# Issuing the loads of v for batches 2 to 7 from ScalarE, with three buffers of their own

## The chip, the cores and the metric

The kernel runs on one core of one Trainium2 chip. The metric is the device time of one execution, in microseconds (us). Profiled executions give a span, from the first to the last instruction; the device time is the span and about 1.7 us.

## The reference

Eight batches, eight heads, 576 positions, 64 features a head, all float32. Attention with a causal mask and a decay bias comes first, then one residual MLP over the joined heads:

```python
scores = scale * q @ k.T                       # per batch and head
cum    = cumsum(max(s, 0))
bias   = min(-(cum[:, None] - cum[None, :]), 0)
attn   = softmax(where(causal, -1e9, scores + bias))
x      = concat_heads(attn @ v)                # [8, 576, 512]
out    = x + relu(layer_norm(x) * g @ w1) @ w2 # 512 -> 2048 -> 512
```

## The kernel before

The kernel is scheduled by hand: every engine runs its instructions in the order in which the program emits them. The program goes through 64 **slots**, one head each. A slot computes the scores of its head, applies the exponential, multiplies with v for the head of two slots before, and fills the rest of TensorE's time with MLP work of the batch before ("units").

v comes in five tiles a batch (four of 128 positions, one of 64). For batches 2 to 7 each tile is loaded as float32 by SyncE and cast to bfloat16 by GpSimd one slot later. k and q of the later batches (rows) go through the same staging buffers: SyncE loads, GpSimd casts, SyncE starts a transposing transfer into `kq`, from which TensorE reads.

```python
stage = ctx.enter_context(tc.tile_pool(name="stage", bufs=6))

def ld_v(b, t):
    ...
    tmp = stage.tile([P, H, D], F32, name="vtmp", tag="st")
    nc.sync.dma_start(
        out=tmp[:pn], in_=v[b, :, t * P : t * P + pn, :].rearrange("h s d -> s h d")
    )
    loaded["v", b, t] = tmp

def cast_v(b, t, eng):                       # on GpSimd, one slot later
    ...
    copy_on(eng, v_bf[b % 2][:pn, t, :, 0:D], loaded.pop(("v", b, t))[:pn])

def ld_rows(gam, t): ...                     # SyncE loads k, q into tag "st"
def tr_rows(gam, t): ...                     # SyncE: dma_start_transpose -> kq

def pre(n):                                  # at the head of slot n
    ...                                      # rows: loads, casts, transposes
    for nb in range(2, B):
        m = n - H * nb + (5 if nb == 2 else 7)
        if 0 <= m < NT:
            ld_v(nb, m)
        if 1 <= m <= NT:
            cast_v(nb, m - 1, "pool")

for n in range(BH):                          # slots from 9 on, cut
    b, h = n // H, n % H
    pre(n)
    ...
    scores(b, h)          # three matmul banks sa, sb, sc; ScalarE Exp after each
    run_units(1, True)    # mlp1: 4 matmuls into ph, then hT by VectorE or ScalarE
    if h % 2 == 0:
        scores_d(b, h // 2)
    run_units(1)
    pv_next()             # attention times v, two slots behind
    ...
    run_units(nu)
```

The softmax here doesn't subtract the row's maximum and nothing guards it: scores larger than these inputs give would overflow.

## Time and profile before

| | before |
|---|---|
| median of the runs given with the kernel | 367.58 us (367.33 to 367.63) |
| profiled execution | 368.54 us, span 366.8 |
| TensorE busy | 355.0 us, 97% of the span |
| loads of v by SyncE | 24 of 256 KB, 6 of 128 KB |
| SyncE's starts of v, shortest / median / longest | 440 / 590 / 1761 ns |

A slot begins with a 512-column matmul into `sa`, so the distance of two such starts is the length of a slot. From slot 24 on, a batch without a stall has slots of 4.63, 4.58, 5.08, 5.02, 4.63, 4.57, 4.63, 4.58 us, and 5.62 in place of 5.02 where the layer norm has a fifth tile. What is over this is a stall.

This is the timeline of TensorE in the kernel before, from 76 to 100 us (start, duration, engine, line, operation, tiles):

```profile
80.58 0.38 PE L312 MATMUL sa<-kq 68*128 68x512 bf16 x1
...
85.20 0.38 PE L312 MATMUL sa<-kq 68*128 68x512 bf16 x1
...
89.78 0.38 PE L312 MATMUL sa<-kq 68*128 68x512 bf16 x1
```

These are slots 20 and 21, of 4.62 and 4.58 us: no stall. (Starts are rounded to 0.01 us, so lengths taken from them can differ by 0.01 from those in the text, which are taken from the unrounded starts.)

### The profile page before, as it was taken

The numbers are of one execution on the slowest core, as the hardware profiler recorded it, in microseconds if no ns is written. First come the engines' busy times: TensorE is split into PE (matmuls) and PEld (weight loads), VectorE is DVE, ScalarE is ACT, GpSimd is POOL, SyncE is SP. The second block draws the span as 40 slices with busy tenths as digits, with TensorE's granted clock in tenths as the row PEclk, the third lists the DMA queues.
The fourth block names the chain that finished last, engine by engine and source line by source line (L and its number), as shares of the span: only waits on it lengthen the run. The fifth ranks groups of instructions, "written<-read, shape, count | busy, mean of one in ns | idle before, by whom it ended". The sixth has DMA issues, their size and how long they took to land.

```text
span 366.8 us, 8315 instructions
## 1 busy us (share of the span) xinstructions
PE 355.0 (97%) x3017; PEld 197.1 (54%) x3067; DVE 202.9 (55%) x535; ACT 191.3 (52%) x367; POOL 164.9 (45%) x447
## 2 busy tenths in 40 slices
PE   8998999999999999999999999999999999999995
PEld 3677555565555555555455555555555554444444
DVE  7697789684357554944384547743675483112211
ACT  5895988467732673367534753476337522501410
POOL 8854468667633656344675563554852101000000
PEclk9999999999999999999999999999999999999999
DMA  8999999999965999599979986798830011011013
GB/s 144 162 195 178 202 211 193 163 240 176 183 146 141 206 199 181 104 215 163 188 176 213 194 183 140 189 191 182 174 102 2 0 59 57 1 58 59 0 31 86
DMA packets 156653, 52.17 MB, mean 142 GB/s; under 512 B 143641, under 2 KB 151940, under 8 KB 156612
## 3 DMA queue, kind: packets, MB, share of 16 engines
q1 hardware_dynamic: 138868, 43.08, 55.5%
q0 software_dynamic: 17344, 8.03, 18.9%
q8 instruction: 24, 0.39, 0.5%
q10 hardware_dynamic: 400, 0.52, 0.4%
q14 instruction: 17, 0.14, 0.2%
HBM read 37.11 MB, written 9.44 MB: 127 GB/s over the span
## 4 chain that ended last, share of the span: by engine, by line
PE 72%; DVE 7%; DMA 6%; SPq 4%; POOL 4%; issue 3%; ACT 3%; POOLq 0%; ACTq 0%
PE py L515 26%; PE ph L497 25%; PE pot L389 6%; SPq L164 3%; PE sc L312 3%; PE sa L312 3%; PE sb L312 3%; DMA rowtmp<-in_q_dram 2%; PE idle L568 2%; DMA vtmp<-in_v_dram 2%; DVE xn L451 2%; PE trx L484 2%; DVE stats L423 1%; POOL er L331 1%; ACT er L323 1%
## 5 line engine op out<-in xcount | busy, mean ns | idle before, releaser
L515 PE MATMUL py<-w_bf,hT 128*128 128x512 bf16 (+1 forms) x565 | 132.1, 373 | 1.6 <-DVE yo L524 0.4
L497 PE MATMUL ph<-xT,w_bf 128*128 128x512 bf16 x478 | 116.4, 379 | 1.1 <-DVE yo L524 0.2
L507 ACT ACTIVATE hT<-ph 128x512 bf16<-128x512 f32 x102 | 61.0, 598 | 64.4 <-PE ph L497 64.4
L515 PEld LDWEIGHTS <-hT 128*128 128x128 bf16 x592 | 53.5, 98 | 49.1 <-issue 0.9
L497 PEld LDWEIGHTS <-w_bf 128*128 128x128 bf16 x560 | 50.1, 97 | 51.3 <-issue 2.9
L323 ACT ACTIVATE er<-sa 128x512 bf16<-128x512 f32 x64 | 38.2, 597 | 70.9 <-PE sa L312 50.1
L331 POOL TENSOR_SCALAR_AFFINE_SELECT er<-er 128x128 bf16<-128x128 bf16 x216 | 59.7, 300 | 22.5 <-ACT er L323 22.3
L505 DVE TENSOR_SCALAR hT<-ph 128x512 bf16<-128x512 f32 x38 | 26.3, 692 | 56.7 <-PE ph L497 49.0
L176 POOL CAST rows<-rowtmp 128x512 bf16<-128x512 f32 (+1 forms) x55 | 33.5, 609 | 50.7 <-DMA rowtmp<-in_q_dram 46.0
L312 PEld LDWEIGHTS <-kq 68*128 68x128 bf16 x452 | 33.4, 97 | 27.4 <-issue 1.7
L389 PEld LDWEIGHTS <-er 128*128 128x128 bf16 x960 | 37.5, 98 | 14.9 <-issue 0.7
L389 PE MATMUL pot<-v_bf,er 128*128 128x65 bf16 x960 | 40.2, 193 | 0.5 <-PE sd L355 0.3
L397 DVE RECIPROCAL rinv<-pot 128x5 f32<-128x5 f32 x64 | 12.3, 192 | 49.2 <-PE pot L389 48.9
L323 ACT ACTIVATE er<-sc 128x512 bf16<-128x512 f32 x64 | 39.2, 612 | 0.0
L323 ACT ACTIVATE er<-sb 128x512 bf16<-128x512 f32 x64 | 38.4, 599 | 0.3 <-PE sb L312 0.2
L524 DVE SCALAR_TENSOR_TENSOR yo<-py,rstd,xb 128x512 f32<-128x512 f32 x32 | 23.9, 748 | 26.2 <-PE py L515 19.7
L399 DVE TENSOR_TENSOR xb<-pot,rinv 128x256 f32<-128x256 f32 x64 | 27.2, 425 | 2.2
L102 POOL CAST v_bf<-vtmp 128x512 bf16<-128x512 f32 (+1 forms) x30 | 18.5, 617 | 19.6 <-DMA vtmp<-in_v_dram 19.5
L439 POOL TENSOR_TENSOR rstd<-rstd,mhalf 128x4 f32<-128x4 f32 (+1 forms) x8 | 8.8, 1095 | 38.0 <-DVE rstd L438 37.9
L312 PE MATMUL sc<-kq 68*128 68x256 bf16 (+1 forms) x216 | 25.3, 229 | 0.3
L423 DVE BATCH_NORM_STATS2 stats<-xb 128x6 f32<-128x128 f32 (+2 forms) x100 | 25.3, 313 | 0.4
L312 PE MATMUL sb<-kq 68*128 68x64 bf16 (+1 forms) x172 | 24.5, 244 | 0.9 <-DMA kq<-rows 0.6
(101 smaller groups left out, 322.1 us busy)
## 6 DMA issues: line engine op xcount, KB each, us to landing
out_dram<-yo SPq DMA_DIRECT2D x32, 256.0 KB
vtmp<-in_v_dram SPq DMA_DIRECT2D x24, 256.0 KB
rowtmp<-in_k_dram SPq DMA_DIRECT2D x44, 128.0 KB
rowtmp<-in_q_dram SPq DMA_DIRECT2D x44, 128.0 KB
w_bf<-in_moe_w_ch_dram POOLq DMA_DIRECT2D x8, 512.0 KB, 10.7
kp<-in_k_dram POOLq DMA_DIRECT2D x9, 144.0 KB, 6.8
qp<-in_q_dram POOLq DMA_DIRECT2D x9, 144.0 KB, 7.0
v_bf<-in_v_dram POOLq DMA_DIRECT2D x8, 128.0 KB, 8.1
```

What stands on the lines that cost most here:

```text
L176: nc.gpsimd.tensor_copy(out=r[0:pn, :, :, 0:D], in_=loaded.pop(("rows", gam, t))[0:pn])
L312: nc.tensor.matmul(a[:, c + a0 - q0 : c + a1 - q0], lhsT=k_cols(b, h, kb), rhs=cols, start=True, stop=not (pe_mask and diag),)
L323: nc.scalar.activation(out=e[:, o : o + 512], in_=a, func=ACT.Exp, scale=scale)
L331: nc.gpsimd.affine_select(out=e[:, o : o + P], in_=e[:, o : o + P], compare_op=ALU.is_ge, fill=0.0, base=0, pattern=[[1, P]], channel_mult ...
L389: nc.tensor.matmul(pot[:, t, :], lhsT=e[:, o : o + P], rhs=vv[:, kb, h, :], start=(kb == 0), stop=(kb == last),)
L399: nc.vector.tensor_tensor(out=xb[b][:, :, hs], in0=pot[:, 0:NF, 0:D], in1=rinv[:, 0:NF].unsqueeze(2).to_broadcast([P, NF, D]), op=ALU.mult,)
L423: nc.vector.bn_stats(out=st[b][:, t, part, :], in_=x[:, lo:hi])
L497: nc.tensor.matmul(ph, lhsT=w1_bf[:, kd, fb * P : (fb + 1) * P], rhs=xT[:, kd, :], start=(kd == 0), stop=(kd == KD - 1),)
L505: nc.vector.tensor_scalar_max(out=hT[:, fb, :], in0=ph, scalar1=0.0)
L507: nc.scalar.activation(out=hT[:, fb, :], in_=ph, func=ACT.Relu)
L515: nc.tensor.matmul(py[0], lhsT=hT[:, fb, t * P : (t + 1) * P], rhs=w2_bf[:, fb, c0:c1], start=(fb == 0), stop=(fb == FB - 1),)
L524: nc.vector.scalar_tensor_tensor(out=yo, in0=py[0], scalar=rs, in1=x[:, c0:c1], op0=ALU.mult, op1=ALU.add)
```

## The change

The intent: take 30 transfer starts from SyncE, whose stream is dense around the transposes of k and q, give them to ScalarE, which is 48% idle, and start the loads sooner, so that GpSimd waits less. The loads get three buffers of their own; `stage`, then for k and q alone, goes from six to four. The casts stay where they are.

```diff
-    stage = ctx.enter_context(tc.tile_pool(name="stage", bufs=6))
+    stage = ctx.enter_context(tc.tile_pool(name="stage", bufs=4))
@@ ld_v
-        tmp = stage.tile([P, H, D], F32, name="vtmp", tag="st")
-        nc.sync.dma_start(
+        tmp = stage.tile([P, H, D], F32, name="vtmp", tag="v", bufs=3)
+        nc.scalar.dma_start(
             out=tmp[:pn], in_=v[b, :, t * P : t * P + pn, :].rearrange("h s d -> s h d")
         )
@@ pre(n)
             m = n - H * nb + (5 if nb == 2 else 7)
-            if 0 <= m < NT:
-                ld_v(nb, m)
             if 1 <= m <= NT:
                 cast_v(nb, m - 1, "pool")
@@ the slot
         scores(b, h)
+        for nb in range(2, B):
+            m = n - H * nb + (5 if nb == 2 else 7)
+            if 0 <= m < NT:
+                ld_v(nb, m)
         run_units(1, True)
```

Below, "the third load" is m = 2 (slots 19, 27, 35, 43, 51 for batches 3 to 7) and "the fifth load" is m = 4 (slots 21, 29, 37, 45, 53).

## The prediction

> **What bounds the kernel now.** I began with the page's busy shares, then read the start of every slot (one head of attention each, 64 in all), the waits around the slots that are too long, SyncE's own stream there, and ScalarE early on. From the page:
>
> ```profile
> PE 355.0 (97%) x3017; PEld 197.1 (54%) x3067; DVE 202.9 (55%) x535; ACT 191.3 (52%) x367; POOL 164.9 (45%) x447
> ```
>
> TensorE is busy 97% of the span, so nothing that only shortens other engines' work moves the end: a change counts only where it opens or closes a gap of TensorE. The page's list of transfers also has 24 loads of v of 256 KB (and 6 of 128 KB), all from SyncE.
>
> Each slot begins with one 512-column score matmul into tile `sa`. The timeline of TensorE from 240 to 262 us, where no stall occurs, and the same view from 160 to 182 us:
>
> ```profile
> 248.21 0.38 PE L312 MATMUL sa<-kq 68*128 68x512 bf16 x1
> ...
> 252.79 0.38 PE L312 MATMUL sa<-kq 68*128 68x512 bf16 x1
> ...
> 257.42 0.38 PE L312 MATMUL sa<-kq 68*128 68x512 bf16 x1
> ```
>
> ```profile
> 170.61 0.38 PE L312 MATMUL sa<-kq 68*128 68x512 bf16 x1
> ...
> 175.95 0.38 PE L312 MATMUL sa<-kq 68*128 68x512 bf16 x1
> ...
> 181.37 0.38 PE L312 MATMUL sa<-kq 68*128 68x512 bf16 x1
> ```
>
> The same two slots of a batch (the last, then the first of the next) take 4.58 and 4.63 us in the first fence, 5.34 and 5.42 us in the second. So 0.76 + 0.79 us is lost there. I laid the other starts from 99 us on beside the same head of the last batch: one more slot is long (4.78 for 4.63, at 156.62 us). Two slots of 5.62 us belong to batches whose layer norm has a fifth tile to transpose; I call those work, not stall. What this part can give back is 0.15 + 0.76 + 0.79 = **1.70 us**.
>
> The waits between 150 and 182 us, largest first in the view, name the stall:
>
> ```profile
> POOL v_bf L102 <- DMA vtmp<-in_v_dram: 3.6, 3, 2.5
> ...
> PEld L312 <- DMA kq<-rows: 1.4, 2, 1.1
> ...
> PEld L389 <- POOL er L331: 0.6, 1, 0.6
> ```
>
> TensorE waits for a transposed tile of k and q (`kq<-rows`), and for a mask that GpSimd (`er`) put on late, because GpSimd, which works in order, stood waiting for a load of v. Both come from SyncE's stream:
>
> ```profile
> 146.33 0.57 SPq L139 DMA_DIRECT2D vtmp<-in_v_dram  x1
> 152.01 0.36 SPq L542 DMA_DIRECT2D out_dram<-yo  x1
> ...
> 167.81 1.73 SPq L139 DMA_DIRECT2D vtmp<-in_v_dram  x1
> 169.66 2.92 SPq L186 DMA_TRANSPOSE kq<-rows  x2
> 172.63 0.62 SPq L139 DMA_DIRECT2D vtmp<-in_v_dram  x1
> 173.67 1.22 SPq L186 DMA_TRANSPOSE kq<-rows  x1
> ```
>
> From 146.9 to 152.0 us SyncE issues nothing: the store of an output tile waits for VectorE, which is in the five tiles of a layer norm. Then it issues almost without a gap until 177 us, and the loads of v stand ahead of the transposes. The transpose that TensorE waits for starts at 173.67, behind a load of v at 172.63 and another at 167.81.
>
> **What the Trainium skill says.** "DMA: Bandwidth & Descriptors", section "Issuing engines are not separate DMA queues": starts from several engines run on the same 16 DMA engines and save only the issuing sequencer's time. The trace can't test it for v yet; but the bytes stay the same, so I count issue time and earlier starts, and no bandwidth. "Perfetto Trace Analysis", section "Sequencer Loop": an engine instruction is pushed into a queue and waits there, while a control instruction is run by the sequencer itself. If a DMA start counts as the latter, part of it hides under an exponential that still runs; no run shows that yet. The same page, section "DMA Instruction — HWDGE (DVE, Sync)": the recorded time of a start is the sequencer's, with a wait for a shared descriptor generator in it, and the movement lies outside. The trace agrees on the last point: the start at 167.81 takes 1.73 us, and the cast that needs its data can run only at 172.37. On sharing, five pairs of stores at the end, from SyncE and ScalarE at once, take 0.47 and 0.50 us each, against 0.36 for a lone store on SyncE: little.
>
> **The change, part by part.**
>
> Removed: 30 starts on SyncE, median 0.59 us (range 0.44 to 1.76) in the view of `vtmp`: 30 x 0.59 = 18 us of SyncE. Between 152 and 174 us four of them take 0.93 + 0.49 + 1.73 + 0.62 = 3.8 us ahead of the late transpose. TensorE waited 1.1 us for it, so that wait should go even if only a third of the 3.8 us is really saved.
>
> Moved: a load now starts when ScalarE has passed the third exponential of its slot. In batches 3 to 7 that is at, for example, 148.0, 153.1, 158.7 and 163.7 us, where SyncE started them at 157.3, 161.3, 167.8 and 172.6: some 8 to 9 us sooner, the first two partly inside the stretch in which SyncE had nothing in flight. GpSimd's 19.5 us of waits for v (16 times in the view of `vtmp`) should mostly end, and with them the 0.6 us wait for the mask. For batch 2 it is the other way: SyncE ran ahead there (29.4, 49.5, 50.0, 55.1, 59.5 us), and ScalarE will come at 49.6, 51.6, 56.1, 59.6 and 64.0. A load took 3.5 to 5 us from start to landing, so GpSimd waits longer there; but the value product of a head comes two slots after its scores, and this slack of about 7 us holds the delay.
>
> Added: 30 starts on ScalarE, an estimate of 0.5 to 0.6 us each, 15 to 18 us. ScalarE has 176 us idle, but not everywhere:
>
> ```profile
> 49.50 0.62 ACT L507 ACTIVATE hT<-ph 128x512 bf16<-128x512 f32 x1
> 49.98 0.63 ACT L323 ACTIVATE er<-sa 128x512 bf16<-128x512 f32 x1
> ```
>
> In this timeline of ScalarE one instruction starts before the last has ended: between 43 and 60 us its idle gaps come to 1.1 us, and it sets the pace. Five starts fall there (slots 11 to 15). Fully exposed they cost 5 x 0.55 = 2.8 us; hidden under the exponential they cost nothing. I take 0.6 us. Later, slots 4 and 5 of a batch run the first MLP product, whose hidden tile ScalarE empties. In slot 37 ScalarE idles 0.26 us after the third exponential, and the TensorE unit that needs the buffer back starts 0.52 us after it was emptied: 0.78 us of slack, above 0.6. A start of over 1 us would cost TensorE some tenths, in ten such slots. I take 0.4 us for the sum. In slots 1 to 3 ScalarE idles about 3 us a slot and the start is free.
>
> Buffers: `stage` goes from six shared to four for k and q alone, v gets three. A gam (one group of four heads) uses five stage tiles in four slots and each is cast one slot after its load, so four suffice.
>
> Sum: -1.7 x 0.85 (one part in seven kept back for what may remain) = -1.45; +0.6 early; +0.4 in the MLP slots; together -0.45 us. I round up the cost a little for its long tail: **366.9 us**.
>
> **The rivals.**
>
> First, ScalarE blocked inside a start. Hardware transfers of the built kernel use eight completion counters in turn, so a start waits for the transfer eight places back. With SyncE 8 us behind, ScalarE could hang on one of its transfers. I took the order of the built program before, put each load behind its slot's third exponential, and compared with the landing of its eighth predecessor in the trace: it had landed at least 1.7 us earlier every time. So against; if it happened in each of five batches at 1 to 2 us, the time would be 373 to 378.
>
> Second, ScalarE becomes the bound: starts of 1 to 2 us beside SyncE's transposes (SyncE's own range goes to 1.76). Ten MLP slots and five early ones at half a microsecond more would make about 371. The short pairs of stores at the end speak against it.
>
> Third, the v loads were hidden anyway and something else keeps the stall: the DMA engines are near full there (share 0.95 to 1.00 in the windows 160 to 180), and a v load in parallel slows k and q. Then 367.6 to 368.6.
>
> Fourth, all goes well and no start shows: 365.9.
>
> **Range and chances.** From 365.4 (all 1.7 us back and a bit in the early slots) to 369.6 (no gain, 2 us lost on ScalarE). Faster by 2% would need 7.35 us; TensorE idles 11.8 us in all, and in the view by stretches of 10 us 4.2 us of it lie before 60 us and 3.8 us at the very end: 0.01. Slower by 2% needs the first rival in most batches: 0.02.
>
> **What would show each step.** Right: the starts at 170.6 and 176 lie 4.6 us apart as everywhere; GpSimd's wait for `vtmp` falls from 19.5 us to under 8; the wait for `kq<-rows` after 60 us is gone; slots 11 to 15 (17.3 us from 46.21 to 63.46) grow by under 1 us; the starts on ScalarE take 0.5 to 0.7 us. Wrong: starts of over 1 us, hidden-layer matmuls that wait for ScalarE, slots 11 to 15 over 1.5 us longer, or new long slots in other batches.

## The result, and the profile after

| | before | after |
|---|---|---|
| median, fast runs of the same rounds | 367.33 us (366.57 to 367.63, 6 runs) | 369.64 us (368.71 to 371.92, 6 runs) |
| profiled execution | 368.54, span 366.8 | 369.04, span 367.3 |
| slots 14 / 21 / 36, us | 4.62 / 4.57 / 4.78 | 4.88 / 5.73 / 5.64 |
| slots 39 / 40, us | 5.34 / 5.42 | 4.58 / 4.63 |

The ratio is 1.0069, with a 95% interval of 1.004 to 1.0099: the same at 2%, but a real loss of 2.3 us in the medians. A ratio here is the mean time of one kernel's fast runs over that of the other's of the same rounds, so it is not quite the ratio of the medians.

The busy line of the page of the kernel after:

```profile
PE 356.9 (97%) x3067; PEld 197.0 (54%) x3067; DVE 202.0 (55%) x535; ACT 191.2 (52%) x367; POOL 161.3 (44%) x447
```

The bound did not change. (The count of matmuls differs because some records of before are missing.) The timeline of TensorE before and after, from 150 to 182 us:

```profile
156.62 0.38 PE L312 MATMUL sa<-kq 68*128 68x512 bf16 x1
...
161.41 0.38 PE L312 MATMUL sa<-kq 68*128 68x512 bf16 x1
```

```profile
157.81 0.38 PE L312 MATMUL sa<-kq 68*128 68x512 bf16 x1
159.03 0.39 PE L312 MATMUL sb<-kq 68*128 68x64 bf16 x3 [0.84 <-DMA kq<-rows]
...
163.45 0.38 PE L312 MATMUL sa<-kq 68*128 68x512 bf16 x1
...
172.65 0.38 PE L312 MATMUL sa<-kq 68*128 68x512 bf16 x1
...
177.23 0.38 PE L312 MATMUL sa<-kq 68*128 68x512 bf16 x1
...
181.86 0.38 PE L312 MATMUL sa<-kq 68*128 68x512 bf16 x1
```

Slots 39 and 40 are clean, 4.58 and 4.63 us, as hoped. But slot 36, which starts at 157.81, now takes 5.64 us instead of 4.63 (4.78 in the profile of before): its second bank, `sb`, waits for a transposed tile. The second new long slot is 21, in the same view from 76 to 100 us:

```profile
80.59 0.38 PE L312 MATMUL sa<-kq 68*128 68x512 bf16 x1
...
85.22 0.38 PE L312 MATMUL sa<-kq 68*128 68x512 bf16 x1
...
90.96 0.38 PE L312 MATMUL sa<-kq 68*128 68x512 bf16 x1
```

Before it took 4.57 us; now 5.73. With slot 14 (+0.26 us) the three add up to 0.26 + 1.16 + 1.01 = 2.43 us.

The waits of the kernel after, all engines, over the whole execution (engine, line, what it waited for: total us, times, longest):

```profile
POOL v_bf L102 <- DMA vtmp<-in_v_dram: 5.7, 5, 2.1
...
PE ph L497 <- ACT hT L507: 1.0, 1, 1.0
...
PE sb L312 <- DMA kq<-rows: 0.8, 1, 0.8
```

GpSimd's waits for v fell from 19.5 to 5.7 us, as forecast, but no gain of that size reached the end. TensorE has one wait of 1.0 us for ScalarE (slot 21) and one of 0.8 us for a transposed tile (slot 36).

**Slot 21.** ScalarE's timeline from 84 to 93 us (ACTq is the sequencer of ScalarE; the bracket is the idle time before an instruction and what the profile holds responsible):

```profile
86.87 0.62 ACT L323 ACTIVATE er<-sc 128x512 bf16<-128x512 f32 x1
88.70 0.65 ACTq L139 DMA_DIRECT2D vtmp<-in_v_dram  x1
89.45 1.09 ACT L507 ACTIVATE hT<-ph 128x512 bf16<-128x512 f32 x2 [1.96 <-DVE xm L406]
```

ScalarE's third exponential ends at 87.49 us, and the next instruction in its program is the start of the fifth load. It begins only at 88.70. Behind it, ScalarE must empty two hidden tiles, and TensorE waits for their buffers. The bracket names VectorE, wrongly: the hidden tiles do not read `xm`. What held the start shows in SyncE's timeline from 76 to 93 us:

```profile
81.72 3.38 SPq L186 DMA_TRANSPOSE kq<-rows  x2
...
87.12 4.85 SPq L186 DMA_TRANSPOSE kq<-rows  x3
92.02 0.58 SPq L164 DMA_DIRECT2D rowtmp<-in_k_dram  x1
```

The second of the two transposes in the first line started at 83.21 us. Its landing, read from the trace's record of the completion count, is at 88.64: 0.06 us before ScalarE's start. In the built program all hardware transfers, of SyncE and ScalarE together, take eight completion counters in turn, and each start first waits until its counter's earlier transfer has landed. The counter of this load had last been given to that transpose. The packed trace also holds the wait itself, a semaphore instruction of line 139 on ScalarE that the views leave out: it lasts from 86.47 to 88.66 us and names two counters, that of the transpose and one whose last landing was long past (85.25). The same holds for the other fifth loads (all from the trace after; "earlier transfer" is the one on the same counter):

| slot | ScalarE's start | earlier transfer, landing |
|---|---|---|
| 21 | 88.70 | transpose, 88.64 |
| 29 | 126.22 | store, 126.12 |
| 37 | 165.70 | row of q, 165.63 |
| 45 | 203.57 | store, 203.51 |
| 53 | 241.67 | row of q, 241.60 |

Five times of five the start comes 0.06 to 0.10 us after the landing. (One fourth load does so too: 81.91 after 81.81, in slot 20, at no cost to TensorE.) In slots 29 to 53 it comes 0.45 to 0.75 us after the begin of the third exponential (0.62 us long), so ScalarE stands for 0.13 us at most before it, and TensorE loses nothing; in slot 21 it comes 1.83 us after, and there TensorE pays.

That a counter is shared in this way fits the Trainium skill, "DMA: Bandwidth & Descriptors", section "Why a DMA increments its semaphore by 16 and not by 1": two transfers in flight on one semaphore can be taken for each other, so each transfer in flight needs its own. With more transfers than counters, someone has to wait, and here it is an engine that computes.

**Slot 36.** SyncE's timeline after, from 150 to 160 us:

```profile
153.66 1.32 SPq L186 DMA_TRANSPOSE kq<-rows  x1
```

ScalarE's, from 150 to 160 us:

```profile
153.16 0.38 ACTq L139 DMA_DIRECT2D vtmp<-in_v_dram  x1
```

And SyncE's in the kernel before, from 140 to 182 us:

```profile
152.46 1.23 SPq L186 DMA_TRANSPOSE kq<-rows  x1
```

This transpose is the one that slot 36 needs. It starts 4.15 us before slot 36 begins; before, it started 4.16 us ahead (152.46 against 156.62). It is not later, it is slower: it landed 5.32 us after its start (158.98, and `sb` starts at 159.03), and before 4.48 us (156.94). What is new beside it is the third load, which ScalarE began at 153.16 and which landed at 158.30; before, SyncE began that load at 157.3.

**ScalarE's starts** themselves are cheap. The view of `vtmp` after (shortest / median / longest ns, first and last start):

```profile
L139 ACTq DMA_DIRECT2D vtmp<-in_v_dram x30: 374/390/722, 46.9 to 241.7; - x30
```

And ScalarE's timeline from 43 to 72 us:

```profile
49.95 0.40 ACTq L139 DMA_DIRECT2D vtmp<-in_v_dram  x1
50.23 0.64 ACT L323 ACTIVATE er<-sb 128x512 bf16<-128x512 f32 x1
50.70 0.65 ACT L323 ACTIVATE er<-sc 128x512 bf16<-128x512 f32 x1
```

The program has this start behind both exponentials, yet it runs at 49.95, ahead of them. That agrees with the Trainium skill, "Perfetto Trace Analysis", section "Sequencer Loop", which the prediction used with a caveat: control instructions are run by the sequencer, while compute waits in a queue. The sequencer ran two instructions ahead.

So I had two suspects: **theory A**, the wait for a completion counter (fifth load, slot 21), and **theory B**, the load begun beside the transpose slows it (third load, slot 36). The rivals: the change of buffers does it; or the starts by ScalarE cost their own time; or the long slots are chance.

### The profile page after: what moved, and what is told of

Same layout as the page of the kernel before. It is cut to its first block, busy times and chain, and to the rows that moved or that the text cites. A ratio compares the mean times of both kernels' runs of the same rounds, so it can differ in the third digit from the quotient of the medians.

```text
span 367.3 us, 8382 instructions
## 1 busy us (share of the span) xinstructions
PE 356.9 (97%) x3067; PEld 197.0 (54%) x3067; DVE 202.0 (55%) x535; ACT 191.2 (52%) x367; POOL 161.3 (44%) x447
## 4 chain that ended last, share of the span: by engine, by line
PE 65%; DMA 11%; issue 6%; DVE 6%; POOL 5%; ACT 3%; SPq 2%; ACTq 0%; POOLq 0%
PE ph L497 26%; PE py L515 24%; PE pot L389 5%; DMA rowtmp<-in_q_dram 3%; DMA kq<-rows 3%; PE sc L312 3%; DMA vtmp<-in_v_dram 3%; PE sb L312 2%; PE sa L312 2%; POOL er L331 2%; ACT er L323 2%; DMA kq<-c 1%; SPq L164 1%; POOL rows L176 1%; PE trx L484 1%
## 5 line engine op out<-in xcount | busy, mean ns | idle before, releaser
L515 PE MATMUL py<-w_bf,hT 128*128 128x512 bf16 (+1 forms) x592 | 136.4, 373 | 0.4 <-DVE yo L524 0.4
L497 PE MATMUL ph<-xT,w_bf 128*128 128x512 bf16 x496 | 117.8, 379 | 1.0 <-ACT hT L507 1.0
L331 POOL TENSOR_SCALAR_AFFINE_SELECT er<-er 128x128 bf16<-128x128 bf16 x216 | 57.8, 291 | 24.0 <-ACT er L323 23.9
L312 PE MATMUL sa<-kq 68*128 68x512 bf16 x64 | 24.4, 381 | 0.4 <-DMA kq<-c 0.3
```

The costliest lines, as they stand in the source:

```text
L312: nc.tensor.matmul(a[:, c + a0 - q0 : c + a1 - q0], lhsT=k_cols(b, h, kb), rhs=cols, start=True, stop=not (pe_mask and diag),)
L331: nc.gpsimd.affine_select(out=e[:, o : o + P], in_=e[:, o : o + P], compare_op=ALU.is_ge, fill=0.0, base=0, pattern=[[1, P]], channel_mult ...
L497: nc.tensor.matmul(ph, lhsT=w1_bf[:, kd, fb * P : (fb + 1) * P], rhs=xT[:, kd, :], start=(kd == 0), stop=(kd == KD - 1),)
L515: nc.tensor.matmul(py[0], lhsT=hT[:, fb, t * P : (t + 1) * P], rhs=w2_bf[:, fb, c0:c1], start=(fb == 0), stop=(fb == FB - 1),)
```

## The experiments

A ratio is given with its 95% interval. Slot lengths are of the one profiled execution of each kernel.

**The two kernels again.** First, how much of this is chance? Both kernels were run unchanged.

> The kernel before, unchanged, to see what its second profile looks like. Theory A (the 1.7 us of long slots between 156 and 181 us are a fixed feature of the kernel): slots 36, 39 and 40 are again 0.15, 0.76 and 0.79 us too long, ratio 1.000. Rival (they were an accident of one execution, which took 368.54 us where the timed ones took 366.6 to 367.6): the slots take 4.63, 4.58 and 4.63 us, the profiled time is about 367.0, ratio 1.000.

Before again: ratio 0.9996 (0.9979 to 1.0014), median 367.30 us. But its profiled execution took 369.0, and its long slots are others: slots 39 and 40 take 4.64 and 4.94 (5.34 and 5.42 in the first profile), 0.41 us lies in slot 48, and 1.3 us in slot 2, where TensorE waits 1.2 us for loads of v.

> The changed kernel, unchanged, for a second profile and the size of the loss. Theory A (ScalarE's start of the fifth load of v in a batch stands waiting for the transfer eight places back, and TensorE then waits for a hidden tile): a slot that holds a fifth load (21, 29, 37, 45 or 53) is again 0.5 to 1.5 us long, the gap of ScalarE before a start ends at the landing of that transfer. Rival (contention of the earlier loads with the transposes): the long slots are those that wait for a transposed tile (36 or such). Ratio 1.005 to 1.010 either way.

After again: ratio 1.0056 (1.0039 to 1.0073), median 369.49 us (before in these rounds 367.45). Slots 14, 21 and 36 take 4.88, 5.37 and 5.58 us: the same three. The five fifth loads again start 0.06 to 0.10 us after the landings of their counters.

What follows: the losses of after repeat, but the stalls of before, from which the prediction took its gain, differ between its two profiled executions.

**The fifth load back on SyncE.**

```diff
-def ld_v(b, t): ... nc.scalar.dma_start
+def ld_v(b, t, eng): ... eng.dma_start
 # pre(n)
+            if m == NT - 1:
+                ld_v(nb, m, nc.sync)
 # behind the scores
-            if 0 <= m < NT:
-                ld_v(nb, m)
+            if 0 <= m < NT - 1:
+                ld_v(nb, m, nc.scalar)
```

> Only the fifth load of each batch goes back to SyncE, to its old place; the other four stay on ScalarE. Theory A (ScalarE blocked at the fifth load): time falls by most of the loss, ratio to before 1.000 to 1.003, no fifth slot is long. Rival (contention of the first four early loads with transposes, or the buffers): it stays, ratio 1.005 to 1.010, slot 36 or others that wait for kq are long.

Ratio 1.0021 (0.9998 to 1.0045), median 367.69. Slot 21 is clean (4.57), slot 36 is as long as ever (5.68), and so is slot 14 (4.89). The interval of the ratio touches 1 and does not reach the 1.0056 of the kernel after; it is the slots that tell the two losses apart. The waits of TensorE have lost the entry for the hidden tile and kept this one:

```profile
PE sb L312 <- DMA kq<-rows: 0.9, 1, 0.9
```

So slot 21 belongs to the fifth load and slot 36 does not.

**ScalarE's loads at the end of the slot.** If the counters are at fault, a later start should find them free.

```diff
         scores(b, h)
-        for nb in range(2, B): ... ld_v(nb, m)
         ...
         run_units(nu)
+        for nb in range(2, B): ... ld_v(nb, m)
 # pre(n): cast one slot later
-            if 1 <= m <= NT:
-                cast_v(nb, m - 1, "pool")
+            if 2 <= m <= NT + 1:
+                cast_v(nb, m - 2, "pool")
```

> ScalarE begins every load at the end of its slot instead of behind the scores, some 2 to 3 us later, and GpSimd casts it one slot later. Theory A: the transfer eight places back has landed by then, ScalarE no longer stands, ratio 0.998 to 1.002. Rival (a start on ScalarE costs by itself, or the loads contend with the transposes): the same starts and nearly the same early transfers remain, ratio 1.004 to 1.010.

Ratio 1.0213 (1.0187 to 1.024), median 374.91: the expectation that the earlier transfers would have landed by then was a miss. ScalarE's timeline of this kernel, from 88 to 96 us:

```profile
92.54 0.69 ACTq L139 DMA_DIRECT2D vtmp<-in_v_dram  x1
93.33 0.60 ACT L323 ACTIVATE er<-sa 128x512 bf16<-128x512 f32 x1 [2.82 <-POOL er L331]
```

ScalarE idles 2.82 us. The transfer on the same counter was a transpose that SyncE had started at 89.30, and it landed at 92.44. Moving the load moved its place in the turn of the counters too, so it inherited a later transfer, and slots 22, 38 and 54 take 6.73, 6.20 and 7.97 us. This speaks for theory A more strongly than what I had expected: the place in the turn decides, and not how late the start comes.

**The buffers alone.** The changed kernel, with SyncE as issuer and the place behind the scores kept.

```diff
-        nc.scalar.dma_start(
+        nc.sync.dma_start(
```

> The change with SyncE issuing: three buffers of their own and four for k and q, the start written behind the scores. SyncE has nothing else between the old and the new place, so its order stays. Theory A (the loss comes from ScalarE issuing): ratio 0.997 to 1.002. Rival (four buffers for k and q are too few, or the separate pools cost): 1.004 to 1.010.

Ratio 1.0013 (0.997 to 1.0055), median 367.76 beside 367.71 of before; two executions took 370.8 and 371.1, both at a granted clock of 0.991, as single executions of several kernels did, before among them (369.84 and 369.9 in these rounds, at 0.995). The profiled one took 366.91 us and has no long slot at all from slot 16 on. Its TensorE timeline from 150 to 182 us:

```profile
156.67 0.38 PE L312 MATMUL sa<-kq 68*128 68x512 bf16 x1
...
161.30 0.38 PE L312 MATMUL sa<-kq 68*128 68x512 bf16 x1
...
175.08 0.38 PE L312 MATMUL sa<-kq 68*128 68x512 bf16 x1
...
179.71 0.38 PE L312 MATMUL sa<-kq 68*128 68x512 bf16 x1
```

Slots 36 and 39 take 4.63 each, and slot 21 takes 4.57. The interval alone would leave room for a loss of 0.5%; the slots do not. The buffers are harmless, and so is the place in the program: with both as in the change, the long slots come only when ScalarE issues. This execution also gives a floor: without long slots the program takes about 366.9 us. The floor is known to some tenths only: take the long slots off the profiled executions of before, after and of the run with the fifth load on SyncE, and 366.8, 366.6 and 366.4 us are left.

**ScalarE with the buffers of before**, the opposite half:

```diff
-    stage = ctx.enter_context(tc.tile_pool(name="stage", bufs=4))
+    stage = ctx.enter_context(tc.tile_pool(name="stage", bufs=6))
-        tmp = stage.tile([P, H, D], F32, name="vtmp", tag="v", bufs=3)
+        tmp = stage.tile([P, H, D], F32, name="vtmp", tag="st")
```

> The change with the old pool: six buffers shared by v, k and q, ScalarE issuing behind the scores. Theory A (ScalarE stands in a start): ratio 1.004 to 1.012, the waits at the fifth load as in the change, perhaps further ones for a buffer. Rival (the loss comes from the buffers): 0.998 to 1.003.

Ratio 1.0386 (1.0351 to 1.0421), median 382.04. It does not separate what it was made for, because something else came in. The largest wait of its TensorE:

```profile
PE trx L484 <- DVE xT L100: 9.6, 4, 3.0
```

In slots 26, 34, 42 and 50 (7.00, 9.28, 7.00, 9.28 us) TensorE's layer norm transposes wait for a copy by VectorE. Which rotating PSUM buffer a tile gets had probably changed with the edit; I have not followed it. The expectation of 1.004 to 1.012 was a miss. What it does show: the third, fourth and fifth loads stand at their counters here as well (a start at 161.40 after a landing at 161.33). And in slot 21, ahead of the disturbed slots, the fifth load starts at 89.90, 0.10 us after the landing of a transpose, and the slot takes 6.10 us: with the buffers of before, slot 21 is long all the same. For the rest the run is confounded and I use it for nothing else.

**The third and the fifth load on SyncE**, the other three on ScalarE.

```diff
 # pre(n)
+            if m in (2, NT - 1):
+                ld_v(nb, m, nc.sync)
 # behind the scores
-            if 0 <= m < NT:
+            if m in (0, 1, 3):
+                ld_v(nb, m, nc.scalar)
```

> The third and the fifth load of each batch go back to SyncE, three stay on ScalarE. Theory A in full (the fifth load makes ScalarE stand, the third lies in front of the transpose that slot 36 needs and costs about 1 us there): slot 36 falls from 5.6 to about 4.7 us, slot 21 stays 4.57, ratio 0.994 to 1.000. Rival (slot 36 is late because SyncE's store waits for VectorE, whoever loads v): slot 36 stays at 5.2 us or more, ratio 1.000 to 1.004.

Ratio 0.999 (0.9954 to 1.0026), median 367.50 beside 367.71. Slot 21 is clean (4.57), slot 36 takes 4.92, that is 0.29 too long instead of 1.01. That lies between what the two theories expected (4.7, and 5.2 or more). Slot 14 is still 4.89. With these two loads back, the loss is gone: the other three loads cost nothing that the times show.

**The third load alone on ScalarE.**

```diff
 # pre(n)
+            if m in (0, 1, 3, 4):
+                ld_v(nb, m, nc.sync)
 # behind the scores
+            if m == 2:
+                ld_v(nb, m, nc.scalar)
```

> One part alone: only the third load of each batch is begun by ScalarE. Theory A (it runs just before the transpose that slot 36 waits for and delays it by about 1 us): slot 36 takes 5.3 to 5.7 us, slots 21, 29, 37, 45, 53 are 4.57; ratio 1.001 to 1.004. Rival (slot 36 was long for another reason, such as SyncE's store): slot 36 at most 4.8 us, ratio 0.998 to 1.001.

Ratio 1.002 (0.9995 to 1.0045), medians 368.20 (367.9 to 368.48) and 367.12; the interval touches 1, so again the slots decide. Slots 14, 21 and 36 take 4.89, 4.57 and 5.66: one load of five brings back all of slot 36. SyncE's timeline of this kernel from 150 to 162 us, and the same transpose in four kernels:

```profile
152.66 1.29 SPq L186 DMA_TRANSPOSE kq<-rows  x1
```

| | transpose starts | lands | took | third load starts |
|---|---|---|---|---|
| before | 152.46 | 156.94 | 4.48 us | 157.3 (SyncE) |
| buffers alone | 152.51 | 156.74 | 4.23 us | 156.55 (SyncE) |
| after | 153.66 | 158.98 | 5.32 us | 153.16 (ScalarE) |
| third load alone on ScalarE | 152.66 | 158.01 | 5.35 us | 152.31 (ScalarE) |

With a load of v begun 0.35 to 0.5 us ahead of it on ScalarE, the transpose takes 0.8 to 1.1 us longer. Slot 36 has no room for it. The other profiles agree: in after again, the fifth back on SyncE and the end of the slot, where ScalarE also begins a load 0.44 to 0.51 us ahead, this transpose takes 5.21 to 5.36 us and slot 36 5.52 to 5.68; in before again, the third and fifth on SyncE and the fifth alone, where none begins there, it takes 4.24 to 4.49 us. Theory B holds. Whether the two share data bandwidth or the making of descriptors, these runs do not tell.

**The fifth load alone on ScalarE.**

```diff
 # pre(n)
+            if 0 <= m < NT - 1:
+                ld_v(nb, m, nc.sync)
 # behind the scores
+            if m == NT - 1:
+                ld_v(nb, m, nc.scalar)
```

> One part alone: only the fifth load of each batch is begun by ScalarE, the first four by SyncE at their old place; own buffers. Theory A (the fifth start stands for a transfer of SyncE eight places back and holds up the exponentials and ReLUs behind it): a slot with a fifth load (21 or one of 29, 37, 45, 53) is 0.5 us or more too long, ScalarE's start begins within 0.15 us of that landing, slot 36 is at most 4.8 us; ratio 1.002 to 1.006. Rival (only all five together make the loss): no long slot, 0.998 to 1.001.

Ratio 1.0004 (0.997 to 1.0038), medians 367.10 and 367.12. I had expected 1.002 to 1.006, and that is a miss. In slot 21 the load now starts at 86.42, before the third exponential, and the slot is clean (4.58). In three of the five batches it still comes 0.06 to 0.07 us after a landing (163.85 after 163.79, 200.76 after 200.70, 239.37 after 239.30), but soon enough: slot 37 loses 0.12 us. With four other loads back on SyncE, the turn of the counters is another. So "the fifth load" is not the cause; its place in the turn in the changed program is.

**Pairs of loads in fewer slots**, all on ScalarE: loads one and two in the first slot, three in the second, four and five in the fourth.

```diff
-            if 0 <= m < NT:
-                ld_v(nb, m)
+            for t in {0: (0, 1), 1: (2,), 3: (3, 4)}.get(m, ()):
+                ld_v(nb, t)
```

> All five loads stay on ScalarE, but the second, third and fifth begin a slot earlier: two starts in the first slot, one in the second, two in the fourth. Theory A: the fifth start no longer stands (its eighth predecessor landed about a slot earlier) and the third lies 5 us ahead of the transpose, so slots 21 and 36 are 4.6 us and the ratio is 0.997 to 1.002. Rival (any start on ScalarE in the middle of a batch stands or contends): 1.004 or more.

Ratio 1.021 (1.0164 to 1.0257), median 374.56: a miss as well. This was meant to step around both waits and met others: starts stand until 123.16 (landing 123.07), 160.58 (160.51), 203.12 (203.02) and 242.78 (242.59), TensorE waits 3.7 us for hidden tiles, and slots 36 and 37 take 6.91 and 6.25. The transpose of slot 36, with the third load a slot further ahead of it, took 4.28 us, as theory B has it; slot 36 is long here because TensorE waits 2.12 us for a hidden tile. A place that is free of such waits cannot be guessed from the time of the load; one has to look up the earlier transfer of its counter.

**GpSimd loads and casts in one transfer**, without ScalarE and without the staging buffers. Two forms were run, both edits of the kernel before.

```diff
 # pre(n), first form
-            if 0 <= m < NT:
-                ld_v(nb, m)
-            if 1 <= m <= NT:
-                cast_v(nb, m - 1, "pool")
+            if 0 <= m < NT:
+                ld_cast_v(nb, m)
```

> Loads of v for batches 2 to 7 begun by GpSimd with the cast in the transfer, as the kernel does for batches 0 and 1: no staging, no cast, no start on SyncE or ScalarE, and other completion counters. Theory A (ScalarE's standing and the eight shared counters make the loss; the loads themselves fit): ratio 0.992 to 1.000, no long slots. Rival (what costs is the contention of the transfers, which stays or grows with 128-byte pieces): 1.003 to 1.015, waits for kq and long slots.

The first form gives a wrong result (relative error 0.175): it writes a tile of v one slot before the last read of the old one. TensorE waited 22.4 us for these loads, and the ratio is 1.085. It is a failed experiment.

```diff
+            if 1 <= m <= NT:
+                ld_cast_v(nb, m - 1)
```

> The loads begun by GpSimd with the cast in the transfer, now at the place of the cast, after the last use of the buffer (the version before this one overwrote it too early, gave a wrong result and made TensorE wait 22 us for the load). Theory: correct; no start on SyncE or ScalarE, no staging, no cast; long slots vanish, ratio 0.995 to 1.001, the floor being the 366.9 us of the execution without long slots. Rival (GpSimd's starts or the small pieces hold up the masks or k and q): 1.003 or more.

The second form is correct, and slower: 1.0095 (1.0052 to 1.0137), median 370.84. The list of GpSimd's waits has

```profile
POOL rows L176 <- DMA rowtmp<-in_q_dram: 52.5, 24, 5.4
```

and 11.8 us for rows of k, against 46.0 and 1.8 us before. The software queue's transfers take 35.0% of the DMA engines' time instead of 18.9%, the rows of k and q come later, and TensorE's wait for `kq<-rows` is 1.4 us instead of 0.6. The long slots did not vanish, so this expectation was a miss too: slots 36 and 40 take 5.65 and 5.33 us. In slot 36 it is the stall of theory B with a third engine as issuer: GpSimd begins a load of v at 151.96, the transpose starts at 151.97 and takes 5.34 us. So it is the load in flight beside the transpose that counts, and not that ScalarE started it. This way of easing SyncE is no better.

## Why the prediction was wrong

It foretold a gain of 0.45 us; a loss of 2.3 us came. The class, "within 2%", held. By its own steps:

1. **TensorE bounds, and GpSimd's and SyncE's relief counts only through its gaps: right.** TensorE stayed at 97%, GpSimd's waits for v fell to 5.7 us (forecast: under 8), and no gain of that size came of it.

2. **"What this part can give back is ... 1.70 us": the size was wrong.** The stall was real in the execution that was profiled, which took 368.54 us while the kernel's timed executions lay at 366.6 to 367.6. From the floor of about 366.9 us, a usual execution of before (about 367.3) holds an estimated 0.4 us of stall, give or take half a microsecond. The profile of before taken again has 0.37 us in slots 39 and 40, not 1.55. The slots were repaired as foretold (4.58 and 4.63 us), but the term of the sum was worth, by this estimate, about −0.4 us and not −1.45.

3. **"It had landed at least 1.7 us earlier every time": wrong, and the main failure.** This dismissed the first rival, which was the right mechanism. The eight-back transfer was counted in the order of the program before. For slot 21 that gave a load of a row of q (started 77.97, landed 80.83), with over 6 us of room. In the built changed program the counters are handed out in an order in which the load stands behind more of SyncE's transfers, among them a row load that in fact starts only at 92.02; its eighth predecessor is then the transpose that lands at 88.64. That transpose also took 5.4 us in after (83.21 to 88.64), against 3.2 us in before (84.62 to 87.78); in after the fourth load, begun by ScalarE at 81.91 and landed at 87.70, was in flight beside it. So the second suspect probably lengthened the wait of the first; no run separates the two in this slot. The rival's size was wrong in the other direction: the start stands in all five batches, but only one of them costs TensorE anything, 1.16 us. The start placed at the end of the slot and the pairs show what the rival costs when it strikes in more batches: 374.9 and 374.6 us, inside the 373 to 378 that the prediction gave it.

4. **The third rival, "a v load in parallel slows k and q": right in mechanism.** The prediction gave it 367.6 to 368.6 and left it out of the sum. The term it lacked is 1.0 us in slot 36, where the transpose takes 5.3 us instead of 4.2 to 4.5. Alone, it gave 368.20, inside its band. The collision stood in the prediction's own numbers: it put a load at 153.1 us and called it partly inside SyncE's quiet stretch, but that stretch ended at 152.0, and the transpose of slot 36, a slot that it counted as already 0.15 us too long, started at 152.46. The sign "the wait for `kq<-rows` after 60 us is gone" failed for this reason: the wait moved from slots 39 and 40 to slot 36.

5. **+0.6 us for slots 11 to 15: too much.** (A reading beside it was off too, without consequence: 13 of the 30 loads of before landed in 3.0 to 3.5 us, where the prediction has 3.5 to 5.) The slots take 17.50 us instead of 17.25, +0.25, all of it in slot 14. The starts took 0.39 us at the median (estimate 0.5 to 0.6) and ran under the exponentials. Slot 14 is 0.26 us longer in every kernel whose third load is on ScalarE at its own place, and in the one with third and fifth on SyncE too, but hardly in the pairs (4.67) and not with all on SyncE or the fifth alone on ScalarE. There TensorE waits 0.8 us for a copy by VectorE where it waited 0.2 for an exponential; that suggests another PSUM buffer, but I did not follow it. **Its cause is open.**

6. **+0.4 us for the MLP slots: the reasoning on slack held where no start was held.** A start of 0.39 us under 0.78 us of slack cost nothing. The warning beside it, "a start of over 1 us would cost TensorE some tenths", was nearest to what came, with the start standing instead of taking long.

Put together after the fact, from the floor of about 366.9 us: no stall left of before's kind, +0.26 (slot 14), +1.16 (slot 21), +1.01 (slot 36) = 369.3 us; measured 369.64, and 369.04 in the profiled execution. The experiments undo it: without the fifth load on ScalarE 367.69, without the third and the fifth 367.50, without ScalarE 367.76. No version beats the kernel before by more than the runs can tell apart.

The citation that served best was "Issuing engines are not separate DMA queues" in "DMA: Bandwidth & Descriptors": moving starts to another engine only saves issue time. Saving it was worth nothing here that the times show, since what TensorE waited for was landings.

## What to carry to other kernels

In this kernel a transfer started from an engine that computes was cheap only where its completion counter came free in time: read from the built program of the change, not of the kernel before, which earlier transfer each start waits for and when that lands in the trace. A load begun sooner is not a gain in itself; ask which transfer on the critical path runs beside it then. And before a stall in one profile is put into a sum as a gain, compare the profiled execution with the timed ones, and profile twice: in this kernel some 1.3 of the 1.7 us, by the estimate above, were not there in a usual execution.

## What the Trainium skill lacked or had wrong

- No page that I read says that a start on a computing engine can stand for the completion counter of another engine's transfer, and that the engine's own compute stands with it. Nearest are "DMA: Bandwidth & Descriptors", "Why a DMA increments its semaphore by 16 and not by 1", and the semaphore wait that "Perfetto Trace Analysis", "DMA Instruction — HWDGE (DVE, Sync)", draws in the sequencer ahead of a start. Here five of five fifth loads started 0.06 to 0.10 us after such a landing, and in slot 21 ScalarE idled 1.96 us and TensorE waited 1.0 us.
- "DMA: Bandwidth & Descriptors", "Issuing engines are not separate DMA queues", says that the transfers interleave and that issuing from several engines saves issue time, but not that it can cost time. Here it cost 2.3 us in the medians (2.0 when repeated).
- The same page has no number for how a load started from another engine slows a transposing transfer: 4.2 to 4.5 us became 5.3 to 5.4 us.
- "Perfetto Trace Analysis", "DMA Instruction — HWDGE (DVE, Sync)": no figure by engine. The same 30 loads took 0.39 us a start at the median on ScalarE and 0.59 us on SyncE. On ScalarE it went by the tile: the fifth loads, of half the size, took 0.61 to 0.72 us, the others 0.37 to 0.44.
